# The first idle matmuls of a fused attention and mixture-of-experts kernel, on a zeroed tile instead of the identity

## The chip, the cores and the metric

The kernel runs on one core of one Trainium2 chip. The metric is the device time of one execution in microseconds (us), taken as the median of several executions. An execution's own time is a little longer than the span of its profile, which reaches from the first to the last instruction.

## What is computed

Three stages follow each other, cut here to what matters:

```python
# attention: B, H, S, D = 2, 8, 576, 64
scores = q @ k.T / sqrt(D), masked causally
local = softmax(scores) @ v
q_p = elu(q) + 1
mem_out = (q_p @ M_prev) / (q_p @ z_prev + 1e-6)
x = g * mem_out + (1 - g) * local          # g = sigmoid(beta), one per head
# dense stage: 1152 tokens, 512 -> 1024 -> 1024 -> 512
x = ((x @ w1) * (x @ w2)) @ w3 @ w_out
# four experts, 512 -> 1024 -> 512
out = sum(p[:, e] * (relu(x @ e_w1[e]) @ e_w2[e]) for e in range(4))
```

The idle matmuls that this document is about compute nothing of this. Their result is written to a PSUM tile that nobody reads.

## The kernel before

The attention stage works on eight pairs of heads, p = 0 to 7. For a pair, `load` (line 196) brings q and k of both heads as tiles `qd` and `kd`, with the feature dimension on the partitions: one head on partitions 0 to 63, the other on 64 to 127. `scores` (line 251) multiplies them on TensorE (PE) in five blocks of query rows, of 128, 256, 384, 512 and 576 key columns. The first four blocks are line 273, where the two heads' halves of the array work beside each other. The fifth, line 262, is one matmul over all 128 partitions in two pieces of 288 columns. For the first four pairs these are plain fp32 matmuls, and each plain fp32 matmul of the program appears in the trace as two weight loads and two matmuls.

`peaks` (line 280) takes each block from PSUM: VectorE (DVE) at line 289 adds the mask and finds the row's extreme (`mn`), ScalarE (ACT) at line 294 takes the exponential into a tile `P`. `trans` (line 319) transposes the P tiles on PE by matmuls with the identity (line 326) and ACT copies them out (line 330). `pv` (line 340) multiplies with v. Beside this the same engines already convert the weights of the dense stage, which come as 64-bit floats: ACT at lines 149 and 150, DVE at 156 and 157, GpSimd (POOL) at 121 and 124.

The order of the work in this stage is written out by hand: a list of names, `FIRST`, of which each name issues one part. It begins with the loads of q and k of pair 0 (`@q0 @k0`), a weight tile (`@w0`), q and k of pair 1, two more weight tiles; then `e0` (the exponential of q, line 236, on ACT), the scores `s00` to `s03`, with `m0x` (DVE) and `x0x` (ACT) between them. Every engine works through its own instructions in that order. SP issues all transfers in order as well; the third load of q, `@q2`, reuses the tile of the first, so it waits until pair 0's scores are done.

Ahead of the list stands a prologue. POOL makes the identity with `make_identity`: a memset and an affine select (lines 197 and 199 of the helper masks.py). It zeroes the mask tile (line 174) between the two, and sets a column of the v tiles (line 193). Then PE runs 13 idle transposes of the identity into the PSUM tile `warm` (lines 206 to 208):

```python
    warm = turn(psM, [P, 512], F32, "M", 2, "warm")
    for _ in range(13):
        nc.tensor.transpose(warm[:, 0:P], identF, identF)
```

The scores of pair 0 come next on PE. They use no output of these transposes; they wait for the landing of q and k, and for PE itself.

Of the kernel before, what the change touches and what calls it, by code (L numbers as in the profile page):

```python
# [8 lines left out]
F32 = mybir.dt.float32  # L9
# [60 lines left out]
def kernel(  # L70
# [16 lines left out]
    nc = tc.nc  # L87
    G, _, S = kT.shape
# [6 lines left out]
    P = 128  # L95
# [3 lines left out]
    SB = S - NB * P  # L99
# [11 lines left out]
    def turn(pool, shape, dtype, tag, bufs, name):  # L111

        n = used[tag] = used.get(tag, -1) + 1
        own = TURNS.get(tag, "")
        return pool.tile(shape, dtype, tag=f"{tag}{own[n] if n < len(own) else n % bufs}", name=name, bufs=1)
# [51 lines left out]
    attn = ExitStack()  # L167
    A1 = attn.enter_context(tc.tile_pool(name="A1", bufs=1, side="right"))
    A2 = attn.enter_context(tc.tile_pool(name="A2", bufs=2, side="right"))
    identF = A1.tile([P, P], F32, name="identF")  # L170
    mask = A1.tile([P, S + P], F32, name="mask")
    bt = A1.tile([P, G // B, NB + 1], F32, name="bt")
# [23 lines left out]
    def load(nm, p):  # L196

        src = {"q": qT, "k": kT}[nm]
        raw_t[nm, p] = t = A2.tile([P, src.shape[-1]], F32, tag=f"{nm}d", name=f"{nm}d{p}")
        nc.sync.dma_start(out=t, in_=src[p])  # L200
# [3 lines left out]
        nc.sync.dma_start(out=v4[n % 4][:, :, 0:D], in_=v[n])  # L204

    warm = turn(psM, [P, 512], F32, "M", 2, "warm")
    for _ in range(13):
        nc.tensor.transpose(warm[:, 0:P], identF, identF)

    parts = {}  # L210

# [18 lines left out]
    def stage_phi(p):  # L230
# [7 lines left out]
        def f1():  # L238
            ex = st["ex"]
            phi_t[p] = phi = A2.tile([P, S], F32, tag="phi", name=f"phi{p}")  # L240
            nc.vector.tensor_scalar(out=ex, in0=ex, scalar1=1.0, scalar2=None, op0=ALU.min)
# [4 lines left out]
    def stage_a(p):  # L246
# [33 lines left out]
        def peaks(qb, low=True, ex=True):  # L280
            for src, i, x in banks[qb]:
                w = src.shape[-1]
                if "mn" not in Pt:
                    Pt["mn"] = A2.tile([P, NS2 + 1], F32, tag="mn", name=f"mn{p}")
                one = Pt["mn"][:, 2 * i + x : 2 * i + x + 1]
                if (i, x) not in Pt:
                    Pt[i, x] = turn(A2, [P, w], F32, f"P{i}", 3 if i < NB else 2, f"P{i}_{2 * p + x}")
                if low:
# [24 lines left out]
    def stage_b(p):  # L313
# [49 lines left out]
        def scaled(dst, ps, eps, gate, nm):  # L363

            r = A2.tile([P, NS2 + 1], F32, tag=f"r{nm}", name=f"r{nm}{p}")
            cuts = (slice(0, NB + 1), slice(NB + 1, NS2 + 1))
            for y, c in zip(ps, cuts):
                nc.vector.scalar_tensor_tensor(
                    out=r[:, c], in0=y[:, :, D], scalar=eps, in1=gate[:, h // 2, 0 : c.stop - c.start],
                    op0=ALU.add, op1=ALU.mult,  # L370
                )
            nc.vector.reciprocal(r, r)
            for y, c in zip(ps, cuts):
                nc.vector.tensor_mul(
                    dst[:, c], y[:, :, 0:D], r[:, c].unsqueeze(2).to_broadcast([P, c.stop - c.start, D])
                )
# [15 lines left out]
        def mem_out():  # L392
            st["m"] = A2.tile([P, NS2 + 1, D], F32, tag="xm", name=f"xm{p}", bufs=1)
            scaled(st["m"], st["n"], 1e-6, gm, "m")
# [1022 lines left out]
```

## Time and profile before

| | |
|---|---|
| median of 3 runs | 670.37 us (668.66 to 670.57) |
| the profiled execution's own time | 668.36 us |
| its span | 666.6 us |
| PE busy | 658.6 us, 99% of the span |
| DVE, ACT, POOL busy | 500.8, 368.6, 293.2 us |
| chain that ended last | PE 89%, DVE 6%, ACT 3% |

The profiled execution is one of its own, beside the three that were timed. The chain that ended last is followed back from the last instruction to whatever released each step. A matmul's duration in the trace is longer than what it adds to a row of matmuls, since they overlap; what one adds is read from the distance between the starts. The profile has a line PEclk for the granted clock of TensorE; the durations of equal matmuls are the other way to see it.

### The profile page before, as it was taken

What the parts mean: (1) busy time and instruction counts of PE and PEld (TensorE: products, weight loads), DVE (VectorE), ACT (ScalarE), POOL (GpSimd) and SP (SyncE); (2) the same over time, 40 slices, a digit from 0 to 9 for tenths busy, and PEclk for the clock granted to TensorE, in tenths of its full rate; (3) what the DMA queues carried; (4) which work ended last, traced back from release to release, by engine and by line L of the source; (5) the groups of instructions that cost most, each with busy time, mean ns of one, the idle gap of its engine ahead of it and who ended that gap; (6) DMA issues with size and microseconds to landing.
All of it is one profiled execution on the core that took longest, in us unless ns stands there. A gap on an engine that the chain in (4) does not pass through costs nothing.

```text
span 666.6 us, 13313 instructions
## 1 busy us (share of the span) xinstructions
PE 658.6 (99%) x5165; PEld 610.9 (92%) x5165; DVE 500.8 (75%) x1021; ACT 368.6 (55%) x780; POOL 293.2 (44%) x307
## 2 busy tenths in 40 slices
PE   8999999999999999999999999999999999999997
PEld 6778899989999999998899998998998999999997
DVE  5989997898849498577777666776767677676766
ACT  6998987757626364365544454355444444444441
POOL 2037646654443121725353545445454534555410
PEclk9999999999999999999999999999999999999999
DMA  8676266534511040120220211211212102111003
GB/s 280 204 250 191 103 202 180 158 116 159 191 65 64 32 157 3 32 95 1 64 64 2 95 32 31 64 32 33 64 33 64 57 8 94 33 33 32 1 32 111
DMA packets 34767, 57.78 MB, mean 87 GB/s; under 512 B 13456, under 2 KB 14480, under 8 KB 34704
## 3 DMA queue, kind: packets, MB, share of 16 engines
q1 hardware_dynamic: 34704, 56.93, 26.8%
q8 instruction: 40, 0.66, 0.4%
q14 instruction: 23, 0.19, 0.1%
HBM read 50.37 MB, written 6.55 MB: 85 GB/s over the span
## 4 chain that ended last, share of the span: by engine, by line
PE 89%; DVE 6%; ACT 3%; issue 1%; DMA 1%; POOL 0%; SPq 0%; DVEq 0%; POOLq 0%; ACTq 0%
PE o L1076 16%; PE Z L1184 15%; PE ob L1125 12%; PE c L608 8%; PE Q L1184 7%; PE ab L558 7%; PE wacc L494 5%; PE Zb L901 4%; PE R L1184 4%; PE pt L326 2%; PE Qb L901 2%; PE sc L273 2%; PE a L349 1%; DVE P L289 1%; PE Rb L901 1%
## 5 line engine op out<-in xcount | busy, mean ns | idle before, releaser
L1076 PE MATMUL o<-w,h 128*128 128x512 f32 x480 | 122.6, 393 | 0.0
L124 POOL TENSOR_TENSOR w<-r,w 128x512 fp32r<-128x512 f32 x48 | 68.1, 1425 | 97.8 <-ACT w L756 97.8
L1076 PEld LDWEIGHTS o<-w,h 128*128 128x128 f32 x480 | 85.3, 188 | 14.6 <-DVE w L127 0.2
L1125 PE MATMUL ob<-w,hS 128*128 128x256 f32 x384 | 55.2, 282 | 0.0
L558 PE MATMUL ab<-xT,ws 128*128 128x288 f32 x384 | 53.5, 297 | 0.0
L608 PE MATMUL c<-hT,W 128*128 128x288 f32 (+2 forms) x384 | 53.2, 295 | 0.0
L558 PEld LDWEIGHTS ab<-xT,ws 128*128 128x128 f32 x384 | 51.4, 188 | 0.7 <-issue 0.2
L608 PEld LDWEIGHTS c<-hT,W 128*128 128x128 f32 x384 | 51.8, 188 | 0.1
L1125 PEld LDWEIGHTS ob<-w,hS 128*128 128x128 f32 x384 | 51.0, 190 | 0.1
L1184 PE MATMUL Z<-X0T,w 128*128 128x320 f32 x288 | 50.4, 310 | 0.3
L494 PE MATMUL wacc<-wo,w3s 128*128 128x512 f32 x192 | 49.8, 403 | 0.0
L1047 ACT ACTIVATE h<-tt 128x320 fp32r<-128x320 f32 x48 | 22.6, 472 | 47.4 <-DVE tt L1220 21.7
L1056 DVE SCALAR_TENSOR_TENSOR acc<-ob,pr,acc 128x256 f32<-128x256 f32 x104 | 44.1, 476 | 5.9 <-PE ob L1125 5.9
L127 DVE TENSOR_TENSOR w<-r,w 128x512 fp32r<-128x512 f32 x64 | 47.1, 747 | 0.0
L1050 DVE SCALAR_TENSOR_TENSOR h<-tt,h 128x320 fp32r<-128x320 f32 x48 | 27.2, 566 | 25.8 <-ACT h L1047 25.8
L1184 PEld LDWEIGHTS Z<-X1T,w 128*128 128x128 f32 x288 | 40.4, 188 | 4.8 <-DVE X1T L127 0.8
L1125 PE MATMUL ob<-w,hA 128*128 128x256 f32 x288 | 44.3, 282 | 0.0
L1184 PEld LDWEIGHTS Z<-X0T,w 128*128 128x128 f32 x288 | 42.9, 188 | 1.1 <-ACT tt L1205 0.7
L1184 PE MATMUL Z<-X1T,w 128*128 128x256 f32 x288 | 42.1, 282 | 0.4 <-DVE X1T L127 0.4
L1205 ACT COPY tt<-Z 128x320 f32<-128x320 f32 (+1 forms) x32 | 12.8, 400 | 53.4 <-PE Z L1184 53.4
L494 PEld LDWEIGHTS wacc<-wo,w3s 128*128 128x128 f32 x192 | 34.3, 188 | 7.9 <-POOL w3s L124 0.8
L1207 DVE TENSOR_TENSOR tt<-tt,Q 128x320 f32<-128x320 f32 (+1 forms) x32 | 14.5, 453 | 35.2 <-ACT tt L1205 35.1
(198 smaller groups left out, 1585.6 us busy)
## 6 DMA issues: line engine op xcount, KB each, us to landing
w3r<-in_moe_w_tiles_dram SPq DMA_DIRECT2D x16, 512.0 KB, 4.0
wr<-in_moe_w_tiles_dram SPq DMA_DIRECT2D x16, 512.0 KB, 4.0
r<-in_moe_w_tiles_dram SPq DMA_DIRECT2D x32, 256.0 KB, 2.9
r<-in_moe_w_dram SPq DMA_DIRECT2D x32, 256.0 KB, 2.9
wor<-in_moe_w_out_dram SPq DMA_DIRECT2D x8, 512.0 KB, 5.1
wf<-tf SPq DMA_DIRECT2D x16, 256.0 KB, 4.2
wr<-wf SPq DMA_DIRECT2D x16, 256.0 KB, 2.9
qd<-in_q_cols_dram SPq DMA_DIRECT2D x8, 352.0 KB, 4.4
```

The source lines that it names most:

```text
L124: nc.gpsimd.tensor_sub(dst, src, r32(hi))
L127: nc.vector.tensor_sub(dst, src, r32(hi))
L494: nc.tensor.matmul(wacc[u], lhsT=w3s[u][:, a, c, :], rhs=wo[4 * g + c][:, bb, :], start=(c == 0 and x == 0), stop=(c == 3 and x == 2),)
L558: nc.tensor.matmul(ps[:, 0:HS], lhsT=self.ws[u][:, wi, kk, :], rhs=xT[b, kk][:, xi, a * HS : (a + 1) * HS], start=(n == 0), stop=(n == 3 * ...
L608: nc.tensor.matmul(st["ps"], lhsT=Wt[kk][:, wi, d * P : (d + 1) * P], rhs=hT[kk][:, xi, t0 : t0 + tw], start=(kk == 0 and x == 0), stop=(k ...
L901: nc.tensor.matmul(st[d], lhsT=b1_set[m][a][:, wi, kk, :], rhs=BX[b][:, xi, kk, :], start=first and kk == 0 and x == 0, stop=(kk == 1 and ...
L1047: nc.scalar.activation(h, src, AF.Relu)
L1050: nc.vector.scalar_tensor_tensor(out=h[:, 1], in0=src, scalar=0.0, in1=r32(h[:, 0]), op0=ALU.max, op1=ALU.subtract)
L1056: nc.vector.scalar_tensor_tensor(out=dst, in0=src, scalar=pr[:, t, e : e + 1], in1=dst, op0=ALU.mult, op1=ALU.add)
L1076: nc.tensor.matmul(ps[0], lhsT=h_of[2 * n + y][x][:, a, i * P : (i + 1) * P], rhs=w2s[q + y][x][:, b, :], start=first, stop=last,)
L1125: nc.tensor.matmul(o_ps[d][:, half], lhsT=h_of[2 * n + y][a][:, ia, half * P : (half + 1) * P], rhs=w2s[q + y][k][:, ib, h * HD : (h + 1) ...
L1184: nc.tensor.matmul(ps, lhsT=w1s[q][a][:, wi, kk, :], rhs=X[c, b][:, xi, kk, :], start=first and kk == 0 and x == 0, stop=(kk == 1 and x == ...
```

## The change

A tile `zw` of 128 x 128 fp32 is added ahead of the identity in the same pool, and VectorE zeroes it. In place of the 13 transposes, PE runs 18 plain fp32 matmuls with `zw` as the weights and 64 of its columns as the moving operand, into the first 64 columns of the same PSUM tile.

```diff
@@ -167,6 +167,8 @@
     A2 = attn.enter_context(tc.tile_pool(name="A2", bufs=2, side="right"))
+    zw = A1.tile([P, P], F32, name="zw")
+    nc.vector.memset(zw, 0.0)
     identF = A1.tile([P, P], F32, name="identF")
@@ -204,8 +206,8 @@
     warm = turn(psM, [P, 512], F32, "M", 2, "warm")
-    for _ in range(13):
-        nc.tensor.transpose(warm[:, 0:P], identF, identF)
+    for _ in range(18):
+        nc.tensor.matmul(warm[:, 0:SB], lhsT=zw, rhs=zw[:, 0:SB], start=True, stop=True)
```

The order of PE's instructions at the start of the program, with the engine that each waits for in brackets, before (`sc` are score blocks, `pt` the transposes of P):

```order
L208 MATMUL warm<-identF 128x128 [waits Pool_49]
L208 MATMUL warm<-identF 128x128 x12
L273 MATMUL sc_0_161<-kd_147,qd_145 128x128 [waits DMAHW1_49,DMAHW0_49]
L262 MATMUL sc_0_192<-kd_147,qd_145 128x288 [waits DVE_49]
L326 MATMUL pt_0_197<-identF,P_1_178 128x128 [waits Activation_49]
```

and in the changed program, where the lines are two higher:

```order
L210 MATMUL warm<-zw 128x64 [waits DVE_49]
L210 MATMUL warm<-zw 128x64 x17
L275 MATMUL sc_0_168<-kd_154,qd_152 128x128 [waits DMAHW1_49,DMAHW0_49]
L264 MATMUL sc_0_199<-kd_154,qd_152 128x288 [waits DVE_49]
L328 MATMUL pt_0_204<-identF,P_1_185 128x128 [waits Activation_49,Pool_49]
```

The idle matmuls wait for DVE instead of POOL, and the wait for POOL's identity has moved to the first transpose of P. On DVE the memset of `zw` stands first, ahead of the tensor-scalar of line 241. Apart from line and buffer numbers nothing else differs on any engine.

## Rows read from the trace of the kernel before

**Rows 1.** The page: the span, the granted clock in 40 slices, the last chain.
```profile
span 666.6 us, 13313 instructions
...
PEclk9999999999999999999999999999999999999999
...
PE 89%; DVE 6%; ACT 3%; issue 1%; DMA 1%; POOL 0%; SPq 0%; DVEq 0%; POOLq 0%; ACTq 0%
```

**Rows 2.** The chain of waits, 0 to 60 us: start, length, what.
```profile
1.93 0.06 POOL v L193
1.98 3.03 PE warm L208 x13
5.02 3.89 PE sc L273 x16
8.91 1.18 PE sc L262 x4
...
10.22 0.64 DVE P L289
...
11.02 0.78 ACT P L294
...
34.60 0.92 PE sc L273 x4
```

**Rows 3.** Timeline of POOL: start, length, instruction, idle time before and releaser.
```profile
0.73 0.20 POOL masks.py:197 MEMSET identF<- 128x128 f32 x1 [0.29 <-POOLq L1377]
...
1.63 0.29 POOL masks.py:199 TENSOR_SCALAR_AFFINE_SELECT identF<-identF 128x128 f32<-128x128 f32 x1
```

**Rows 4.** Timeline of PE, several windows between 4.5 and 10 us.
```profile
4.59 0.42 PE L208 MATMUL warm<-identF 128*128 128x128 f32 x1
4.95 3.96 PE L273 MATMUL sc<-kd,qd 64*128 64x128 f32 x16
...
5.32 0.85 PE L273 MATMUL sc<-kd,qd 64*128 64x128 f32 x4
...
5.54 1.06 PE L273 MATMUL sc<-kd,qd 64*128 64x256 f32 x4
...
7.67 1.24 PE L273 MATMUL sc<-kd,qd 64*128 64x512 f32 x4
...
8.31 0.59 PE L273 MATMUL sc<-kd,qd 64*128 64x512 f32 x2
8.84 1.24 PE L262 MATMUL sc<-kd,qd 128*128 128x288 f32 x4
```

**Rows 5.** Tiles `warm` and `sc`, four windows: ns min/median/max, first and last start.
```profile
L208 PE MATMUL warm<-identF x13: 421/421/476, 2.0 to 4.6; 128*128 128x128 f32 x13
...
L273 PE MATMUL sc<-kd,qd x2: 580/580/580, 4.9 to 5.0; 64*128 64x128 f32 x2
...
L273 PE MATMUL sc<-kd,qd x4: 417/499/580, 4.9 to 5.3; 64*128 64x128 f32 x4
...
L262 PE MATMUL sc<-kd,qd x4: 406/406/510, 8.8 to 9.7; 128*128 128x288 f32 x4
```

**Rows 6.** Groups by shape, 4.9 to 8.7 us, then 10.8 to 12.6 us: busy us, mean ns.
```profile
L273 PE MATMUL sc<-kd,qd 64*128 64x384 f32 x4 | 1.5, 844 | 0.0
...
L273 PE MATMUL sc<-kd,qd 64*128 64x384 f32 x4 | 0.8, 482 | 0.0
```

**Rows 7.** Timeline of DVE and ACT, 3.8 to 11.1 us.
```profile
3.83 0.68 ACT L236 ACTIVATE ex<-qd 128x576 f32<-128x576 f32 x1 [1.82 <-DMA qd<-in_q_cols_dram]
4.55 0.46 DVE L241 TENSOR_SCALAR ex<-ex 128x576 f32<-128x576 f32 x1 [4.55 <-ACT ex L236]
5.04 0.76 DVE L242 SCALAR_TENSOR_TENSOR phi<-qd,ex 128x576 f32<-128x576 f32 x1
6.76 0.29 DVE L289 CUSTOM_DVE_ANT_0 P<-sc,mask 128x128 f32<-128x128 f32 x1 [0.96 <-PE sc L273]
...
7.09 2.55 ACT L294 ACTIVATE P<-P,mn 128x128 f32<-128x128 f32 x6 [2.58 <-DVE mn L289]
...
10.22 0.76 DVE L289 CUSTOM_DVE_ANT_0 P<-sc,mask 128x576 f32<-128x576 f32 x1 [1.25 <-PE sc L262]
...
11.02 0.78 ACT L294 ACTIVATE P<-P,mn 128x576 f32<-128x576 f32 x1 [0.23 <-DVE mn L289]
```

**Rows 8.** Busy time of PE, PEld, DVE, ACT, POOL in two stretches.
```profile
10.22:22.00 11.78, 11.49 (x126) 8.15 (x126) 11.40 (x42) 11.55 (x26) 1.90 (x2) 1.00 0.86 273
...
34.60:60.00 25.40, 25.36 (x241) 20.49 (x242) 22.19 (x60) 22.83 (x43) 14.15 (x12) 1.00 0.66 217
```

**Rows 9.** Timeline of SP; then tile `kd`, 0 to 20 us, issue to landing.
```profile
1.17 0.42 SPq L200 DMA_DIRECT2D kd<-in_k_cols_dram  x1
...
10.15 0.33 SPq L200 DMA_DIRECT2D qd<-in_q_cols_dram  x1
...
DMA to landing us min/median/max: 3.3/5.4/6.1
```

## The prediction

> **What bounds the kernel now.** I read the page first: PE holds 89% of the chain that ended last, so time is gained or lost where that chain is [rows 1]. The chain of waits then shows that the change touches its very first links: POOL, the 13 idle transposes from 1.98 us, the 20 score records of pair 0, then DVE and ACT in turn, and PE again from 34.60 us [rows 2]. From there PE is busy 25.36 of 25.40 us [rows 8], so a head that ends earlier or later moves the end by as much. In the head, ACT and DVE are the full engines: 11.55 and 11.40 of 11.78 us [rows 8]. What counts is therefore when they get their first scores.
>
> Three readings of the timeline give the prices. First, the scores wait for PE, not for data: kd is issued at 1.17 and lands 3.3 us later, at 4.5 [rows 9]. The last idle transpose starts at 4.59, adds 0.21 and so ends at 4.80; the first score record starts at 4.95 [rows 4], a handover of 0.14 us. Second, the clock. The page shows full PEclk from the start [rows 1], but the durations deny it: a 384-column score takes 844 ns in pair 0 and 482 in pair 1 [rows 6]. Two 128-column pairs of score records start 0.22 us apart (5.32 and 5.54, rows 4), 1.67 ns a column, while the 288-column records of line 262 start 0.243 apart ((1.24 − 0.41 − 0.10) / 3; rows 4, 5), 0.84 ns a column. [...] The first 512-column pair has 0.64 us (7.67 to 8.31, rows 4), halfway between 0.85 and 0.43, so the clock rose near 8.1, after six microseconds of matmuls of which the first 2.8 were transposes. Third, a weight load that nothing hides: the first score record takes 580 ns and the next 417, so its load costs 0.163 us at 1.2 GHz; at 2.4 GHz 510 − 406 = 0.104; for an idle transpose 476 − 421 = 0.055 [rows 5].
>
> **The change part by part.** *Start.* POOL's identity needs its memset at 0.73 and its select until 1.92 [rows 3]. DVE is free until 4.55 [rows 7]. Its memset has no row; POOL's of the same shape takes 0.20 us [rows 3] and DVE's costlier 128 x 128 step 0.29 [rows 7], so `zw` is ready at 0.93 to 1.02 and PE starts at 1.0, a second earlier. DVE's later work doesn't feel it.
>
> *Removed:* 13 transposes, 0.214 us each ((4.59 − 1.98 − 0.05) / 12; rows 2, 4).
>
> *Added:* 18 fp32 matmuls, which are 36 loads of 128 columns and 36 streams of 64. A stream is half a 128-column one, 0.107 us at 1.2 GHz. No row shows a short stream behind a full load. If loads hide wholly behind streams, a record costs 0.107; if nothing overlaps, 0.163 + 0.107 = 0.270. The trace shows loads starting beside the stream before them, so I take the longer of the two: the load, 0.163, and 0.104 at 2.4 GHz.
>
> [...]
>
> *The clock.* Where it rises isn't in the program. Today 2.8 us of idle transposes ended without it, and it came during the scores, which are plain matmuls [rows 4, 5]. I take it that plain idle matmuls do what the scores did, and that it rises within or soon after them: between 4.8, where the idle work ends today, and 8.1, where it rises today; in the middle, 6.4. [...]
>
> *Sum.* From 1.0 to 6.4 us 33 records at 0.163 run; three more at 0.104 end at 6.7; with the handover the scores start at 6.85, 1.9 us later than now. They run at 2.4 GHz throughout. DVE's first step now comes 1.81 us after the scores start (4.95 to 6.76, rows 7); 768 columns at 0.84 instead of 1.67 ns and a load at 0.10 instead of 0.16 take 0.70 off. It comes at 6.85 + 1.11 = 7.96, 1.20 late. ACT starts behind it and has 3.70 us of work before the 576-column exponential (7.09 to 11.02 less 0.23 idle, rows 7), which it reaches at 11.99 instead of 11.02: **0.97 us late**. PE's own end of pair 0 is less late: line 273 takes 2.33 us (2,560 columns, a load, a handover) instead of 3.90, line 262 its 1.24, so DVE's 576-column step comes at 10.56 instead of 10.22, and SP's next load of q [rows 9] moves by the same 0.34. ACT, the later, sets the head. 668.36 + 0.97 = **669.3 us**.
>
> With the rise at 4.8 the idle stream ends at 6.15 and ACT is 0.41 late: 668.8. With the rise at 8.1 it ends at 6.87, the first scores run cold, and ACT is 1.66 late: 670.0. The likeliest case's own range is 668.8 to 670.0.
>
> *At no cost:* the wait for POOL at the first transpose of P (identity done at 1.92, that transpose runs near 9.9), and the PSUM tile, which has the same user before and after.
>
> **Against the median.** The sum stands on an execution 2.0 us faster than the median of 670.37. Such scatter is what a clock that rises later in other executions would make: a rise only after pair 0's scores would cost ACT about 1.6 us. If so, the earlier rise narrows the scatter and the sum needs no offset; that is argued, not shown. With the offset it would be 671.3. A measurement here can tell about 0.3%, 2.0 us, from no change: faster is below 668.4, slower above 672.4.
>
> **Rivals.** *Loads hide (0.107 us each).* The idle stream ends at 4.85, the scores start at 4.99 as now. With the clock up by then DVE starts 0.66 earlier, ACT gains that and its 0.23 of idle: 667.5. With the rise at 8.1 nothing changes: 668.4. For it: loads elsewhere do run beside streams; against: the 163 ns. *Zeros and short streams don't raise the clock.* Then the scores start at 7.01 and the rise slides with them: everything 2.07 late, 670.4. For it: no row shows how the clock answers to a row of short matmuls on zeros; against: the scores raised it as plain matmuls. *No overlap, and slower.* At 0.270 a record, with the rise at 6.4, 20 run cold and 16 at 0.158; scores start at 9.07, ACT is 3.2 late: 671.6. With no rise they start at 10.86: 674.0. Against it: in every row of matmuls in this trace loads lie beside streams. It decides for slower from 0.24 us a record on, where the scores start at 9.88 and 0.70 comes back.
>
> **How the numbers follow.** Forecast 40%: nearly all within 0.3% of the median, 4 points below. Hidden loads 27%: 22 points faster, 5 same. No effect on the clock 20%: 18 same, 2 slower. No overlap 8%: 3 same, 5 slower. Something else 5%: 1, 3, 1. Faster 0.27, same 0.65, slower 0.08. The range runs from the hidden-loads case, rounded down to 667.4, to the forecast with the median's whole offset, 671.4.
>
> **What would show it.** PE's first record near 1.0 us, 36 records about 0.16 apart, the first score near 6.9 and its 384-column records at 482 ns; DVE's first step near 8.0 and ACT's 576-column exponential near 12.0. Records 0.107 apart and a score at 5.0 mean the first rival; 844 ns again at 384 columns mean the second; a score after 9 the third. An ACT step that comes a microsecond later while the end doesn't move would break the step that carries the head to the end.

## The result, and the profile after

The changed kernel takes 674.86 us (median of 6 runs, 674.06 to 676.71); the kernel before, run beside it, 669.93 (6 runs, 668.66 to 670.75). The ratio is 1.0084, 95% interval 1.0070 to 1.0097: slower by 0.8%, outside the predicted range. The profiled execution of the changed kernel took 675.19 us, against 668.36 before.

The page of the changed kernel, its span and granted clock:

```profile
span 673.4 us, 13361 instructions
...
PEclk9999999999999999999999999999999999999999
```

PEclk again shows full speed from the start, as in [rows 1], and again the durations deny it, as the rows of `warm` and `sc` below show. No run shows a frequency: what the texts on record call 1.2 and 2.4 GHz are two paces of PE, 1.67 and 0.84 ns a column of a score, or 844 and 482 ns for a record of 384 columns [rows 6]. That these are two levels of its clock is the author's reading, and they are called cold and warm below. The chain of waits of the changed kernel (start, length, what), which answers to [rows 2]:

```profile
0.83 0.17 DVE zw L171
1.04 7.95 PE warm L210 x36
8.99 1.61 PE sc L275 x8
10.74 0.29 DVE P L291
11.07 2.50 ACT P L296 x6
```

The idle stream starts 0.94 us earlier, as meant, and is the longest link of the head: 7.95 us where the transposes had 3.03. DVE and ACT now come into the chain with their first scores. The timeline of PE and PEld, DVE, ACT and SP of the changed kernel, which answers to [rows 3, 4, 7, 9]:

```profile
1.04 7.76 PEld L210 LDWEIGHTS warm<-zw 128*128 128x128 f32 x36 [1.04 <-DVE zw L171]
1.04 7.95 PE L210 MATMUL warm<-zw 128*128 128x64 f32 x36 [1.04 <-DVE zw L171]
8.92 3.63 PE L275 MATMUL sc<-kd,qd 64*128 64x128 f32 x16
10.74 0.29 DVE L291 CUSTOM_DVE_ANT_0 P<-sc,mask 128x128 f32<-128x128 f32 x1 [5.24 <-PE sc L275]
11.07 2.50 ACT L296 ACTIVATE P<-P,mn 128x128 f32<-128x128 f32 x6 [6.86 <-DVE mn L291]
13.79 0.33 SPq L202 DMA_DIRECT2D qd<-in_q_cols_dram  x1
13.87 0.76 DVE L291 CUSTOM_DVE_ANT_0 P<-sc,mask 128x576 f32<-128x576 f32 x1 [0.98 <-PE sc L264]
14.67 0.78 ACT L296 ACTIVATE P<-P,mn 128x576 f32<-128x576 f32 x1
```

The scores start at 8.92 us instead of 4.95. DVE's first step comes 3.98 us late, ACT's first exponential 3.98 late, its 576-column one 3.65 late (14.67 against 11.02) and the next load of q 3.64 late. DVE waited 5.24 us for PE, ACT 6.86 us for DVE: nothing but the idle stream is in their way. Tile `warm` by durations (ns minimum, median, maximum; first and last start), and behind it tile `sc` in a window that ends at 10.45 us:

```profile
L210 PEld LDWEIGHTS warm<-zw x36: 288/333/338, 1.0 to 8.5; 128*128 128x128 f32 x36
L210 PE MATMUL warm<-zw x36: 421/421/472, 1.0 to 8.6; 128*128 128x64 f32 x36
...
L275 PE MATMUL sc<-kd,qd x4: 631/738/844, 9.9 to 10.4; 64*128 64x256 f32 x2, 64*128 64x384 f32 x2
```

First: 36 records in 7.95 us, the last 0.42 long and the first 0.05 longer than the others, so they start (7.95 − 0.42 − 0.05) / 35 = **0.214 us apart**, where I had 0.163. Second: all durations are alike up to the last, and behind the stream the 384-column records still take 844 ns, as in pair 0 before [rows 6]. PE stayed cold through 7.7 us of idle matmuls, and the clock rose only during the scores, whose 512-column records take 590 ns (1057 where all are cold, in the second profile below).

### The profile page after: what moved, and what is told of

It reads as the page before. It is cut to its first block, busy times and chain, and to the rows that moved or that the text cites. A ratio compares the mean times of both kernels' runs of the same rounds, so it can differ in the third digit from the quotient of the medians.

```text
span 673.4 us, 13361 instructions
## 1 busy us (share of the span) xinstructions
PE 663.9 (99%) x5188; PEld 616.0 (91%) x5188; DVE 502.4 (75%) x1022; ACT 368.6 (55%) x780; POOL 291.3 (43%) x307
## 4 chain that ended last, share of the span: by engine, by line
PE 84%; DVE 6%; ACT 5%; DMA 3%; issue 1%; SPq 0%; DVEq 0%; ACTq 0%
PE o L1078 16%; PE Z L1186 15%; PE ob L1127 12%; PE c L610 7%; PE Q L1186 7%; PE ab L560 5%; PE wacc L496 5%; PE R L1186 4%; PE Zb L903 3%; PE a L351 2%; PE pt L328 2%; DMA wr<-in_moe_w_tiles_dram 2%; PE Qb L903 1%; ACT P L296 1%; PE warm L210 1%
## 5 line engine op out<-in xcount | busy, mean ns | idle before, releaser
L296 ACT ACTIVATE P<-P,mn 128x128 f32<-128x128 f32 (+4 forms) x72 | 37.4, 586 | 6.9 <-DVE mn L291 6.9
```

The source lines that it names most:

```text
L296: nc.scalar.activation(Pt[i, x], Pt[i, x], AF.Exp, bias=one, scale=-1.0)
```

## The experiments

Ratios are medians against the kernel before, run in the same series, with 95% intervals. "Own" is the profiled execution's own time.

**The tile alone.** `zw` and its memset stay, the 13 transposes of the identity come back.

```diff
-    for _ in range(18):
-        nc.tensor.matmul(warm[:, 0:SB], lhsT=zw, rhs=zw[:, 0:SB], start=True, stop=True)
+    for _ in range(13):
+        nc.tensor.transpose(warm[:, 0:P], identF, identF)
```

> The zeroed tile and its memset on VectorE are added, but the 13 idle transposes of the identity stay. Theory of length (the scores of pair 0 stand behind a longer idle stream): the first score starts at 4.9 to 5.0 us as before, and the time is that of before, ratio 0.998 to 1.002. Rival, placement (the new tile moves every later tile of its side of SBUF, and that is what costs): ratio 1.006 to 1.009 with the scores at 4.9.

669.35 us against 669.23, ratio 1.0003 (0.9993 to 1.0013); scores at 4.94. Tile, memset and the shift of what lies behind them in memory cost nothing. The loss is in the matmuls.

**Half as many.**

```diff
-    for _ in range(18):
+    for _ in range(9):
```

> The change with 9 idle matmuls instead of 18. Theory of length: 18 records at 0.213 us end near 4.9, the first score starts at 5.0, and the time is that of before within 1.2 us, ratio 0.998 to 1.002. Rival, kind (zeros leave the clock at 1.2 GHz for longer than transposes do): 384-column score records still at 844 ns in pair 0 and the fifth block, 288 columns, at 1.2 GHz too (about 0.48 us between starts instead of 0.24), 1.5 us slower or more, ratio 1.002 to 1.004. Rival, placement: ratio 1.006 to 1.009.

Ratio 1.0008 (0.9994 to 1.0021), 669.63 us: nine matmuls fewer take the loss away. Timeline of PE and DVE:

```profile
1.05 4.10 PE L210 MATMUL warm<-zw 128*128 128x64 f32 x18 [1.05 <-DVE zw L171]
5.08 4.64 PE L275 MATMUL sc<-kd,qd 64*128 64x128 f32 x16
...
11.32 0.76 DVE L291 CUSTOM_DVE_ANT_0 P<-sc,mask 128x576 f32<-128x576 f32 x1 [2.22 <-PE sc L264]
```

The records keep their price (18 in 4.10 us) and the scores start almost where they did. But line 275 now takes 4.64 us instead of 3.96 [rows 4], all of it cold (the 512-column records at 1057 ns), and DVE's 576-column step is 1.1 us later than in [rows 7]. So behind this stream, which ends where the 13 transposes ended, the clock rose later (in line 264's records, the first of them still at 797 ns) than in any of the three profiles of the kernel before. The profiled execution took 671.33 us, though, the second longest of the ten with a median of 669.63, so the later rise needn't be what the others had.

**Half the load.** The weights are 64 columns of `zw`; the stream is unchanged.

```diff
-        nc.tensor.matmul(warm[:, 0:SB], lhsT=zw, rhs=zw[:, 0:SB], start=True, stop=True)
+        nc.tensor.matmul(warm[0:SB, 0:SB], lhsT=zw[:, 0:SB], rhs=zw[:, 0:SB], start=True, stop=True)
```

> The change with 64 columns of weights instead of 128 in each of the 18 idle matmuls, 64 columns streamed as before. [...] If load and stream run one after the other, a record costs about 0.16, the first score starts near 7.0 and the ratio is 1.002 to 1.005. [...]

Timeline of PE and DVE, and tile `warm`:

```profile
1.04 4.10 PE L210 MATMUL warm<-zw 128*64 128x64 f32 x36 [1.04 <-DVE zw L171]
5.07 2.43 PE L275 MATMUL sc<-kd,qd 64*128 64x128 f32 x16
...
8.82 0.76 DVE L291 CUSTOM_DVE_ANT_0 P<-sc,mask 128x576 f32<-128x576 f32 x1 [0.49 <-PE sc L264]
...
L210 PE MATMUL warm<-zw x36: 314/314/367, 1.0 to 4.8; 128*64 128x64 f32 x36
```

The same 36 records take half the time, 0.107 us apart ((4.10 − 0.31 − 0.05) / 35) and not the 0.16 of a load and a stream one after the other: the **load's columns** set the pace, and the stream had not changed. And with zeros, back to back, the scores run warm from their start (2.43 us instead of 3.96, 482 ns at 384 columns). This is the first rival's price per record (0.107) without its gain: DVE's 576-column step is 1.4 us earlier than before, but the whole takes 669.53 us, ratio 1.0009 (0.9998 to 1.0021).

**As many transposes as fill the same time.** No `zw`, 32 transposes of the identity.

```diff
-    for _ in range(18):
-        nc.tensor.matmul(warm[:, 0:SB], lhsT=zw, rhs=zw[:, 0:SB], start=True, stop=True)
+    for _ in range(32):
+        nc.tensor.transpose(warm[:, 0:P], identF, identF)
```

> The kernel before with 32 idle transposes of the identity instead of 13, so that the idle stream ends near 8.8 us as in the change, by the other kind of matmul and without the new tile. Theory of length: the first score starts at 8.9, ACT's first exponential near 11.1, ratio 1.006 to 1.009, as the change. Rival, kind: the same length of transposes costs less than the change, ratio under 1.005, because the clock is up earlier. Rival, placement: ratio near 1.000.

672.25 us, ratio 1.0057 (1.0038 to 1.0077): this long stream costs too, but less than expected. In the profiled execution the scores start at 6.95, not at 8.9, because the transposes sped up on the way. Tile `warm` in two windows, 1.9 to 4.6 us and 5.1 to 6.9 us:

```profile
L208 PE MATMUL warm<-identF x13: 354/421/476, 2.0 to 4.6; 128*128 128x128 f32 x13
...
L208 PE MATMUL warm<-identF x18: 272/272/273, 4.9 to 6.7; 128*128 128x128 f32 x18
```

The duration falls from 421 to 272 ns between 4.6 and 4.9 us, some 2.8 us after the first transpose. **Here the clock rose with nothing but transposes before it.**

**Before and after once more**, beside the others.

> The kernel before, unchanged, for a second profile. If the first profile stood at the early end of its own scatter because of waits behind 70 us (every other profile so far loses about 0.7 us between 70 and 95 us against it), this one loses it too, and its own time is 669 to 670. If the moment at which the clock rises is what scatters, its rise lies between 4.7 and 8.1 us and its first 576-column step on VectorE moves with it, between 8.5 and 10.3 us.

> The change, unchanged, for a second profile. Theory: 36 records at 0.213 us, all at 1.2 GHz, first score at 8.9, and a rise of the clock at 11 us or later, since the idle records do not bring it; VectorE's 576-column step at 13.8 us or up to 1.6 us later. Rival, that the rise in the first profile was late by chance: a rise inside the idle stream, with records at about 0.105 behind it.

Before: 1.0011 (1.0000 to 1.0022), own 667.92. After: 1.0078 (1.0058 to 1.0099), own 675.38. In both executions of the changed kernel the scores start alike, at 8.92 and 8.91, but in the second all of line 275's run cold. Timeline of its PE and DVE:

```profile
1.04 7.94 PE L210 MATMUL warm<-zw 128*128 128x64 f32 x36 [1.04 <-DVE zw L171]
8.91 4.64 PE L275 MATMUL sc<-kd,qd 64*128 64x128 f32 x16
...
15.20 0.76 DVE L291 CUSTOM_DVE_ANT_0 P<-sc,mask 128x576 f32<-128x576 f32 x1 [2.26 <-PE sc L264]
```

DVE's 576-column step comes at 15.20 instead of 13.87: the moment of the rise moves the head by 1.3 us from one execution to the next.

**No idle matmul at all.** `zw` and the loop are gone.

```diff
-    zw = A1.tile([P, P], F32, name="zw")
-    nc.vector.memset(zw, 0.0)
...
-    for _ in range(18):
-        nc.tensor.matmul(warm[:, 0:SB], lhsT=zw, rhs=zw[:, 0:SB], start=True, stop=True)
```

> No idle matmul at all. Theory: the scores wait for their data alone and start at 4.5 to 4.7 us, all at 1.2 GHz at first; the clock rises 3 us or more behind that. Ratio 0.998 to 1.003. If the 13 transposes are worth something by raising the clock, this is slower than before by up to 1 us (ratio 1.000 to 1.003) although its scores start 0.3 earlier; if they are worth nothing, ratio 0.998 to 1.000.

```profile
4.70 4.64 PE L271 MATMUL sc<-kd,qd 64*128 64x128 f32 x16 [4.70 <-DMA kd<-in_k_cols_dram]
...
11.46 0.76 DVE L287 CUSTOM_DVE_ANT_0 P<-sc,mask 128x576 f32<-128x576 f32 x1 [2.73 <-PE sc L260]
```

In this timeline of PE and DVE the scores start on the landing of kd at 4.70 and all of line 271's run cold. 670.77 us, ratio 1.0025 (1.0007 to 1.0042): the 13 transposes are worth 1.6 us in the median, although with them the scores start 0.24 us later. That they earn it by an earlier rise of the clock fits this profile, but the profiled execution was one of the longer ones (673.08; the ten range from 669.49 to 674.00). The 18 zero matmuls cost 4.9.

**The same 18 matmuls on the identity.**

```diff
-        nc.tensor.matmul(warm[:, 0:SB], lhsT=zw, rhs=zw[:, 0:SB], start=True, stop=True)
+        nc.tensor.matmul(warm[:, 0:SB], lhsT=identF, rhs=identF[:, 0:SB], start=True, stop=True)
```

> 18 idle matmuls as in the change, but on the identity that POOL makes (no zeros, no new tile), so that they start at 2.0 us. Theory of load and stream: the data does not matter, 36 records at 0.213 us, first score near 9.9, clock at 1.2 GHz through the idle stream, ratio 1.008 to 1.011. Rival, zeros: with ones in the data the clock rises inside the stream, the records behind it come every 0.105 us, first score between 6 and 8, ratio 1.001 to 1.005.

676.58 us, ratio 1.0106 (1.0091 to 1.0121). Timeline of PE:

```profile
1.97 7.94 PE L208 MATMUL warm<-identF 128*128 128x64 f32 x36 [1.97 <-POOL v L193]
9.84 4.64 PE L273 MATMUL sc<-kd,qd 64*128 64x128 f32 x16
```

With ones in the data the stream has the same length, 7.94 us, and line 273's scores behind it run cold to their last. So the zeros are not at fault.

**The same 18 matmuls, twice the stream.** 128 columns are streamed behind each 128-column load.

```diff
-        nc.tensor.matmul(warm[:, 0:SB], lhsT=zw, rhs=zw[:, 0:SB], start=True, stop=True)
+        nc.tensor.matmul(warm[:, 0:P], lhsT=zw, rhs=zw, start=True, stop=True)
```

> The change with 128 columns streamed in each idle matmul instead of 64: the same 36 loads at the same 0.213 us, but the stream now fills the whole record instead of half. If the change's idle records leave the clock at 1.2 GHz because half of each is the load alone, the clock rises here inside the idle stream, 3 to 7 us after its start, records behind it come every 0.105 to 0.11 us, the first score starts at 6 to 8 us at 2.4 GHz, and the ratio is 1.002 to 1.006. Rival, that fp32 idle matmuls with a full load do not raise it whatever they stream: first score at 8.9 and at 1.2 GHz, ratio 1.006 to 1.009.

Timeline of PE, and tile `warm` in two windows, 1.0 to 5.2 and 5.7 to 7.3 us:

```profile
1.05 6.42 PE L210 MATMUL warm<-zw 128*128 128x128 f32 x36 [1.05 <-DVE zw L171]
7.39 2.43 PE L275 MATMUL sc<-kd,qd 64*128 64x128 f32 x16
...
L210 PE MATMUL warm<-zw x19: 421/421/582, 1.0 to 5.0; 128*128 128x128 f32 x19
...
L210 PE MATMUL warm<-zw x16: 275/275/314, 5.5 to 7.2; 128*128 128x128 f32 x16
```

The pace before the rise is that of the changed kernel, 19 records from 1.0 to 5.0, though twice as many columns are streamed: at 64 columns, counted at 1.67 ns each, half of each record of 0.214 us was a load with nothing beside it. And here the clock rises, between 5.0 and 5.5, within the idle stream. This pair (36 loads of 128 zero columns, the stream at 64 or at 128) differs in its source in nothing but the columns streamed. With 64 the stream stayed cold to its last record, in all three profiles of the changed kernel and in the one on the identity (36 records in 7.94 or 7.95 us); with 128 the clock rose on the way, from 421 to 275 ns a record, in the one profile there is. 674.20 us, ratio 1.0054 (1.0035 to 1.0074; single executions from 671.71 on). That is more than its head explains: DVE's 576-column step comes at 11.14, 0.9 us later than in [rows 7]. In the profiled execution, of 674.98 us, the clock also fell for a while in the middle (last section), which brings its mean granted clock down to 0.997. The other four have 0.999 to 1.000, and two of those still took 674.20 and 674.41, so that fall isn't what makes this kernel slow.

**A stream that ends when kd lands.** Eight full matmuls, meant as a version that beats both.

```diff
-    for _ in range(18):
-        nc.tensor.matmul(warm[:, 0:SB], lhsT=zw, rhs=zw[:, 0:SB], start=True, stop=True)
+    for _ in range(8):
+        nc.tensor.matmul(warm[:, 0:P], lhsT=zw, rhs=zw, start=True, stop=True)
```

> 8 idle matmuls on the zeroed tile, 128 columns streamed: 16 records at 0.213 us, from 1.0 to 4.5 us, about where the first scores' data lands. Theory: first score at 4.6 to 4.8 us, clock up 0 to 3 us behind it, so that the head ends up to 1.5 us earlier than before's; ratio 0.997 to 1.000. Rival, that waits behind 70 us take back what the head gains, as in the run with half the load: ratio 0.999 to 1.002.

Timeline of PE and DVE:

```profile
1.04 3.78 PE L210 MATMUL warm<-zw 128*128 128x128 f32 x16 [1.04 <-DVE zw L171]
4.87 2.60 PE L275 MATMUL sc<-kd,qd 64*128 64x128 f32 x16
...
8.79 0.76 DVE L291 CUSTOM_DVE_ANT_0 P<-sc,mask 128x576 f32<-128x576 f32 x1 [0.51 <-PE sc L264]
```

Scores come as early as before, nearly all warm (line 275 in 2.60 us, in 2.43 where all are), and DVE's 576-column step 1.4 us earlier than in [rows 7]. Yet the kernel takes 668.56 us against 669.11, ratio 0.9994 (0.9985 to 1.0003), which can't be told from no change.

**Before and after a third time**, to see whether the losses late in the program come back.

> The kernel before once more, for a third profile. If the waits between 70 and 130 us that every other kernel's profile shows (0.3 to 0.8 us of idle PE) are scatter of the executions, this one may show them, and then its time is 669 to 670; if they come from a head that ends at another moment than before's, it shows none, as the first two, and its span is 666 to 667 again.

> The change once more, for a third profile. First score at 8.9 us, VectorE's 576-column step between 13.8 and 15.4, so that the head is 3.6 to 5.2 us late against the first profile of before. If what is lost behind 70 us is scatter, it differs from the 3.2 and 1.9 us of the first two profiles and may be under 1; if it belongs to the change, it is 1.5 to 3.5 again.

Before: 0.9984 (0.9960 to 1.0007), own 667.76. After: 1.0083 (1.0054 to 1.0113), own 674.12, DVE's 576-column step at 13.75. Timeline of its PE:

```profile
1.04 7.94 PE L210 MATMUL warm<-zw 128*128 128x64 f32 x36 [1.04 <-DVE zw L171]
8.92 3.52 PE L275 MATMUL sc<-kd,qd 64*128 64x128 f32 x16
```

So there are three profiles of either kernel. Landmarks for following the head to the end are ACT's exponentials of q, one for each pair (line 236, after the change 238). The start of each in us; all are single rows of ACT's timeline:

| kernel | pair 1 | pair 2 | pair 3 | pair 4 | pair 5 | pair 6 | pair 7 | own time |
|---|---|---|---|---|---|---|---|---|
| before | 19.3 | 25.3 | 44.9 | 51.0 | 82.6 | 115.1 | 161.0 | 668.36 |
| after | 23.0 | 29.1 | 48.7 | 54.2 | 87.1 | 120.4 | 166.1 | 675.19 |
| before, second | 18.9 | 24.9 | 44.5 | 50.1 | 82.6 | 114.7 | 160.6 | 667.92 |
| after, second | 24.3 | 30.4 | 50.0 | 56.4 | 88.6 | 121.8 | 167.4 | 675.38 |
| before, third | 18.9 | 24.9 | 44.5 | 50.1 | 82.6 | 114.8 | 160.6 | 667.76 |
| after, third | 22.9 | 28.9 | 48.5 | 54.2 | 87.1 | 119.7 | 165.4 | 674.12 |
| eight full matmuls | 18.3 | 24.3 | 43.9 | 50.0 | 82.0 | 115.1 | 160.8 | 668.56 |

In the three comparisons the head is 3.7, 5.4 and 4.0 us late at pair 1, and 3.8, 5.5 and 4.0 late at pair 3: it is carried whole, as predicted, to pair 3. At pair 4 the three are 3.2, 6.3 and 4.1 late, nearly the same in sum. Own times differ by 6.8, 7.5 and 6.4, so another 2.1 to 3.1 us go missing behind that. Two places show in the busy windows (PE, PEld, DVE, ACT, POOL) of the changed kernel, between its landmarks of pairs 5 and 6 and from pair 7 on:

```profile
87.10:120.40 33.30, 32.65 (x344) 31.03 (x343) 28.36 (x72) 25.80 (x53) 16.26 (x16) 1.00 0.58 187
166.00:205.00 39.00, 37.77 (x379) 36.34 (x378) 24.00 (x52) 19.56 (x41) 16.01 (x15) 1.00 0.36 118
```

And of the kernel before, in the same stretches of its program:

```profile
82.60:115.10 32.50, 32.50 (x346) 31.23 (x347) 27.36 (x71) 25.53 (x52) 16.72 (x16) 1.00 0.63 191
161.00:200.00 39.00, 38.98 (x390) 37.76 (x388) 25.09 (x52) 19.81 (x41) 17.16 (x16) 1.00 0.39 128
```

Before, PE never idles in the first of them and for 0.02 us in the second; after, for 0.65 and 1.23. The second has a single large wait, in PE's timeline of the changed kernel:

```profile
188.28 0.66 PE L328 MATMUL pt<-identF,P 128*128 128x128 f32 x4 [1.20 <-DVE asb L574]
```

The kernel with eight full matmuls is 0.6 to 1.0 us ahead of the three of before at pair 1, and level or 0.4 behind at pair 6: from 82.0 to 115.0 us its PE is busy for 32.22 of 33.00 us, and there its lead is gone. The kernel with the tile alone, whose head is no later than that of the kernel before, loses as much there: between its own landmarks of pairs 5 and 6, at 82.53 and 115.71, PE is busy for 32.43 of 33.18 us.

## Why the prediction was wrong

**The term that failed first: the price of a record.** The prediction took "the longer of the two: the load, 0.163". That it chose the load was right, its size was not: 0.214 us measured cold, 0.107 for half the columns. The 0.163 was a difference of durations (580 − 417 in [rows 5]), which shows only what of a load stuck out in front of one stream. [Rows 2, 4] held a nearer neighbour: the idle transposes, of 128 columns loaded and 128 streamed, were 0.214 us apart. That row can't tell whether the load or the stream set this pace, so 0.214 was a price that the range had to allow for. With 0.214 and my rise at 6.4 us, 26 records start cold (the last at 1.04 + 25 × 0.214 = 6.4) and end at 6.6; ten more at about 0.107 end at 7.7, and with the handover the scores start at 7.8 instead of 6.85. ACT is then 0.97 + 0.97 = 1.9 late: 670.3. This term alone would have left the forecast within 0.3% of 668.36 and inside the range.

**The step that failed with it: "plain idle matmuls do what the scores did".** They didn't at this shape. The whole stream stayed cold in all three profiles of the changed kernel (36 records in 7.94 or 7.95 us), so the ten records at the end cost twice as much, and then the scores paid cold prices too. That makes 36 × 0.214 = 7.7 us from 1.04, scores at 8.9 instead of 7.8, and the head 3.65 us late. 668.36 + 3.65 = 672.0 would have been the sum. The zeros weren't the reason (the second rival's), since with the identity in their place the stream stayed cold as well (7.94 us). What differs is the shape: each record of 0.214 us streams 64 columns, 0.107 us at 1.67 ns each, and spends as long again on its load alone. With 128 columns streamed behind the same loads the clock rose at 5.0 to 5.5 us, and with half the load it was up when the scores started at 5.07, in one profile each. By what rule the clock answers to a record's shape no run shows. Nor had the scores done it alone: without any idle matmul they ran cold for all of line 271 (4.64 us).

**Transposes and plain matmuls.** The prediction set the two apart: 2.8 us of idle transposes ended without a rise, and it came during the scores, which are plain matmuls. No transpose row of the kernel before could show whether more of them would have brought it too, since its stream ended at 4.80; the 32 transposes did: 421 to 272 ns after 2.8 us of nothing but transposes. Taking the 13 out left line 271's scores cold to their end in the profiled execution, and cost 1.6 us in the median. The prediction's upper value, 670.0 for a rise at 8.1, still took the records at 0.163.

**What held.** `zw` at 1.00 and PE at 1.04 (predicted 0.93 to 1.02 and 1.0), and the tile alone at no cost. The handover: the last idle record starts at 8.57 (8.99 − 0.42), adds 0.21, and the first score comes 0.14 later, at 8.92. The head: DVE's 576-column step 3.65 late, ACT's exponential 3.65 late. And "a head that ends earlier or later moves the end by as much" held to pair 3, near 50 us.

**What it left out.** Behind 50 us the own times part by another 2.1 to 3.1 us. The medians part by 4.9, less than the profiled executions, because all three profiled executions of before (667.76 to 668.36) are faster than its medians (668.6 to 669.9). If the unprofiled executions have the heads of the profiled ones, some 4 of the 4.9 us are the head; part of the rest is idle time of PE that appears in the busy windows above. Why the changed kernel meets it in each of three profiles and the kernel before in none was not settled. The kernel whose head was early met it between pairs 5 and 6 too, and so did the one with the tile alone, so it isn't lateness as such; the last section has what goes with it there. A fitting guess, not shown, is that the kernel before meets it in those of its executions that were not profiled. The prediction's reading of its scatter as the clock's moment holds in part: the three profiles of before have their 576-column step at 10.22, 9.65 and 9.72, and the latest has the longest own time (668.36 against 667.92 and 667.76); but that is 0.6 us of the 2 that it was to explain.

**The rivals.** Hidden loads fell with the 0.214. "Zeros and short streams don't raise the clock" was right about the clock and named the short streams, but priced it with 0.163 a record: at 0.214 its 2.07 us become about 3.9. "No overlap" had the right sign and place (scores at 9.07) from a wrong price: 0.214 is a load by itself with the stream hidden under it, and its 0.24 as the point of decision, (9.88 − 1.0 − 0.14) / 36, took the idle stream as cold to its end but the scores behind it as warm (the 0.70 that comes back), where the first of them ran cold too. Its 674.0 for the case with no rise lies near the measured 674.86 by luck: it puts the scores at 10.86, where they started at 8.92, and has nothing of what is lost behind pair 3. The two unknowns were treated as independent, and the case in which both go wrong together had no chance of its own. Here they went together: the record in which the load sets the pace, and the stream fills half of it, was the one behind which the clock stayed down.

## What to carry to other kernels

Count an idle stream in loads as well as in columns: a plain fp32 matmul here is two loads and two streams, and with loads of 128 columns a cold record cost about 0.214 us whether 64 or 128 columns were streamed behind them, so the shorter moving operand saved nothing. An idle stream that is to warm the clock is best checked by the durations behind it, and let end when the first data land: here 8 matmuls with 128 columns streamed behind each load of 128 took 3.8 us, and nearly all scores behind them ran warm (line 275 in 2.60 us), where 18 with 64 streamed took 7.9 and ended cold. Follow an early gain along landmarks before counting on it: 0.9 to 1.4 us won at DVE's 576-column step were gone at 115 us.

## What the runs showed that I had not expected

**The half-filled records left the clock down.** 7.7 us without a gap between records ended cold, 0.214 us from start to start, where in the run with 32 transposes the clock rose after 2.8 us of them. PE's busy time doesn't show the difference: it is 7.74 us in the 7.74 from 1.04 to 8.78, since the records, 0.42 us long, overlap.

**The clock fell in the middle.** In the profiled execution with twice the stream, busy windows (PE, PEld, DVE, ACT, POOL, then the granted clock) and PE's timeline:

```profile
254.70:258.20 3.50, 3.50 (x18) 3.50 (x16) 3.50 (x7) 0.98 (x2) 1.82 (x2) 0.51 0.00 0
...
253.52 1.06 PE L903 MATMUL Zb<-BXT,b1w 128*128 128x288 f32 x6 [2.21 <-ACT u L913]
...
255.61 1.64 PE L903 MATMUL Qb<-BXB,b1w 128*128 128x288 f32 x6
...
258.33 0.96 PE L903 MATMUL Qb<-BXT,b1w 128*128 128x288 f32 x6
```

PE had waited 2.21 us for ACT, and from 254.7 us on the granted clock stood at 0.51 for 3.5 us: six records of 288 columns take 1.64 us in it and 0.96 behind it. That the wait brought the fall is not shown.

**Of two steps that DVE and POOL start together one takes longer, and it can be either.** Near 82.7 us both start a two-input step within 30 ns. In the kernel with the tile alone:

```profile
82.66 1.29 POOL L124 TENSOR_TENSOR ws<-tf,ws 128x512 fp32r<-128x512 f32 x1
82.68 1.81 DVE L127 TENSOR_TENSOR wo<-tf_wo,wo 128x512 fp32r<-128x512 f32 x1
```

And in the second profile of the kernel before:

```profile
82.69 1.86 POOL L124 TENSOR_TENSOR ws<-tf,ws 128x512 fp32r<-128x512 f32 x1
82.71 0.69 DVE L127 TENSOR_TENSOR wo<-tf_wo,wo 128x512 fp32r<-128x512 f32 x1
```

One of them takes longer: DVE 1.81 us instead of 0.69, or POOL 1.86 instead of 1.29. After POOL's end DVE runs 82.68 + 1.81 − 83.95 = 0.54 us in the first pair, after DVE's end POOL runs 82.69 + 1.86 − 83.40 = 1.15 us in the second, somewhat less than the 0.69 and 1.29: as if the longer step made little way until the other had ended. That is the author's estimate from these sums; what holds it up is not shown. The recorded starts don't tell which of the two will be the longer, since POOL's is 20 ns ahead in both.

Eight profiles sort by which of the two is the longer. In four (two of the changed kernel, the tile alone, eight full matmuls) DVE's step takes 1.81 or 1.82 us, and between pairs 5 and 6 PE idles for 0.65 to 0.78 us; in four POOL's takes 1.86, and PE idles for 0 to 0.20. The latter four are the three of the kernel before and the third of the changed kernel:

```profile
87.20 1.86 POOL L124 TENSOR_TENSOR ws<-tf,ws 128x512 fp32r<-128x512 f32 x1
87.22 0.68 DVE L127 TENSOR_TENSOR wo<-tf_wo,wo 128x512 fp32r<-128x512 f32 x1
```

So DVE's long step goes with the loss between pairs 5 and 6. That it causes it wasn't tried, and the losses behind pair 7 come in the third profile of the changed kernel as well, where POOL's step was the long one.
